# Attention, dense mixture and routed mixture on one core: the turn to the routed mixture is rearranged

## The chip, the cores and the metric

One core of a Trainium2 chip runs one program. TensorE (PE) multiplies, VectorE (DVE), ScalarE (ACT) and GpSimd (POOL) do the elementwise work, and SyncE (SP), ACT and POOL issue the DMAs. The metric is the device time of one execution in microseconds (us); less is better.

## What is computed

Three layers follow each other. Causal attention with a decay (batch 2, 8 heads, 576 positions, 64 per head) gives x, 1152 tokens of 512 numbers. A dense mixture runs every token through 4 experts. A routed mixture sends each token through at most one of 8 experts:

```python
def _moe_ref(x, domain_probs, w1, w2):            # N 1152, D 512, E 4, F 1024
    p = domain_probs / (domain_probs.sum(-1, keepdims=True) + 1e-09)
    for e in range(E):
        h = np.maximum(x @ w1[e], 0.0)
        out += p[:, e:e + 1] * (h @ w2[e])

def _moe2_ref(x, w_skip, w_gate, w1, w2):         # N 1152, D 512, E 8, F 1024
    do_compute = x @ w_skip > 0
    out = x.copy()
    xc = x[do_compute]
    e_idx = np.argmax(xc @ w_gate, axis=1)
    gate_w = softmax(xc @ w_gate)[rows, e_idx]
    for e in range(E):
        h = np.maximum(xc[e_idx == e] @ w1[e], 0.0)
        y[e_idx == e] = gate_w[...] * (h @ w2[e])
    out[do_compute] = xc + y
```

## The kernel before

**The stages.** Attention takes the first 200 us or so, the dense mixture runs until about 520, the end of the routing until 527, and the routed mixture until 628, where the last results go out by an indirect DMA.

**The dense mixture** works through 8 units u (an expert and a half of F, numbered 0 to 7), each for two groups of tokens: group g=0 holds tokens 0 to 511, g=1 the other 640. The up product (emit_up, L749 to L807) is a product of seven sums in the manner of Strassen; each operand of x is split in a high and a low half, `xsh[g]` and `xsl[g]`, which lie in SBUF for all units. The down product (emit_down L832, down_block L809 to L830) adds each block of 128 tokens into the accumulator `acc`; a quarter of a block is three matmuls `dn` (L818 to L820), and DVE adds the finished block to acc (L830).

**The last unit's down product** (L901) is mixed with the routing. The table `plan` (L836 to L841) names, for block n and quarter j, which step of the routing of which block t of tokens is emitted there. route1 issues ACT's stores of the finished block of acc into the DRAM buffers `xd` and `out` and, for t under 5, `xda` (store, L639 to L643), then transposes the block on PE (`xp`, L648) and copies it on ACT (`xt`, L649). route2 computes the logits on PE (`lg`, L655) and chooses the expert on DVE. route3 counts earlier tokens per expert on PE (`pf`, L683 and L685) and makes the slots and the one-hot matrix on DVE (L687 to L698). route4 adds the tokens into the slots' lists (`pids`, L704) and computes the weight of the choice on ACT (L716). `lg` and `pf` share a place in PSUM. The plan has a regular spacing for blocks 0 to 3 and entries of its own for blocks 4 to 7. ACT's stores use a ring of DMA lanes, so that a store also waits for an earlier one on its lane.

**The routed mixture's weights** are blocks of 1 MB (128 x 2048). SP loads most of them (`load_m`, L140 to L144, tiles `wm`) and POOL a few by indirect DMA (L1035 to L1042). The list `mpool` says which memory block i goes to, on a ring of 17: 0 is a free buffer of the dense weights (loaded with unit 7), 1 to 10 lie over the sums, weights and x operands of the dense up product, and 11 to 16 over other buffers of the dense mixture. load_m(1, 13) stands after unit 7's up product, when the pools of that memory are closed.

**The routed mixture** has per expert a tile of 64 slots (`Few`) and two further tiles for what is left over (`Many`). Zeroed rows `xe_1` to `xe_7` and `xo_0`, `xo_1` (L983 to L988) are filled from `xd` by POOL's indirect gathers (L592), whose empty slots keep the zeros. The first tile's rows `xs0` are gathered earlier from `xda`. Per tile, PE transposes the rows (`tpx`, L1054), ACT or DVE copies them (`xt`), PE multiplies up (L1061), ACT applies the relu (`hs`, L1064), PE transposes (`tp`, L1068) and multiplies down (`yp`, L1076). The zeroed rows lie over the memory of acc, so that their first writes wait until the stores of acc are done.

Of the kernel before, what the change touches and what calls it, by code (L numbers as in the profile page):

```python
# [7 lines left out]
F32 = mybir.dt.float32  # L8
# [10 lines left out]
P = 128  # L19
# [11 lines left out]
NS7 = 7  # L31
# [15 lines left out]
def kernel(  # L47
# [16 lines left out]
    def pool(stack, name, bufs=1, side="left", space=None):  # L64
        kw = dict(space=space) if space is not None else dict(side=side)
        return stack.enter_context(tc.tile_pool(name=name, bufs=bufs, reuse_waits="tile", **kw))

    const = pool(ctx, "const")
    dram = ctx.enter_context(tc.tile_pool(name="dram", bufs=1, space=DRAM))
    wrawu = pool(ctx, "wrawu", 1)  # L70
    upst = ExitStack()
    sumsp = pool(upst, "sums", 1)
    w1p = pool(upst, "w1a", 1)
# [26 lines left out]
    dps = const.tile([P, NB, E1], F32, name="dps")  # L100
    dsum = const.tile([P, NB], F32, name="dsum")
    wgs = const.tile([P, KD, E2 + 1], F32, name="wgs")
    xsh, xsl = [[xtp.tile([P, NS7, 2, GW[g]], F32R, name=f"x{c}_{g}") for g in range(2)] for c in "hl"]
    xtail = xop.tile([P, KD, S - 2 * GW[0]], F32, name="xtail")

    xd = dram.tile([N, DM], F32, name="xd")
# [33 lines left out]
    def load_m(i0, i1, eng=SY):  # L140
        for i in range(i0, i1):
            if chunks[i][1] < E2:
                w, a, e, h = ring(i)
                eng.dma_start(out=w, in_=(m1, m2)[a][e, h])  # L144

    def sub(eng, out, a, b):
        eng.tensor_tensor(out=out, in0=a, in1=b, op=ALU.subtract)  # L147
# [49 lines left out]
    with ExitStack() as at:  # L197
# [207 lines left out]
        def x_src(g, i, k):  # L405
            return x_parts(g, i, k // 2)[:, k % 2] if k in (0, 2, 3) else state["t", g, i][(4, 5, 1, 6).index(k)]

        def x_high(g, i, *ks):
            for k in ks:
                A.copy(out=xsh[g][:, k, i, :], in_=x_src(g, i, k))  # L410

        def x_low(eng, g, i, *ks):
            for k in ks:
                sub(eng, xsl[g][:, k, i, :], x_src(g, i, k), xsh[g][:, k, i, :].bitcast(F32))

        def x_sums(eng, g, i):
            t = xop.tile([P, 4, GW[1]], F32, tag="t", name=f"xs_{g}_{i}")
# [173 lines left out]
    def gather(xe, ix, table=xd, blocks=NB):  # L591
        G.indirect_dma_start(out=xe, out_offset=None, in_=table.rearrange("n (g c) -> (n g) c", g=2),  # L592
                             in_offset=bass.IndirectOffsetOnAxis(ap=ix, axis=0),
                             bounds_check=2 * blocks * P - 1, oob_is_err=False)

    outr = out.rearrange("n (g c) -> (n g) c", g=2)
    accp = pool(ctx, "accp", 1, "right")
    w1ps.append(pool(ctx, "w1b", 1, "right"))
    wrawd = pool(ctx, "wrawd", 1, "right")
    w2p = pool(ctx, "w2p", 1, "right")  # L600
    onehot = accp.tile([P, NB, P], BF16, name="onehot")
    xs0 = accp.tile([P, HD], F32, name="xs0")
    xt0 = accp.tile([P, HD], F32, name="xt0")
    pida = accp.tile([P, E2], F32, name="pida")
    idx0 = accp.tile([P, 1], I32, name="idx0")
    cnt = accp.tile([P, E2], F32, name="cnt")
    G.memset(xs0, 0.0)
    load_d(0)
    with tc.manual_schedule():
# [15 lines left out]
    UL = len(units) - 1  # L625

    with ExitStack() as mo:
        acc = pool(mo, "acc", 1, "right").tile([P, NB, DM], F32, name="acc")
        rt_p = pool(mo, "rt", 2, "right")
        hid_p = pool(mo, "hid", 1, "right")  # L630
        mid_p = pool(mo, "mid", 2, "right")

        macc = {}
        rt = {}
# [112 lines left out]
        hid = {}  # L747

        def emit_up(u, g, q, jobs):  # L749
            w, xh, xl, wt = GW[g], xsh[g], xsl[g], ws["u", u, q]  # L750
            hh, hl = hid[u, g]

            def bank(nm):
                return ps_p.tile([P, 512], F32, tag="ps", name=f"{nm}_{u}_{g}_{q}")[:, :w]

            def product(ps, a, b):
                for i in range(2):
                    T.matmul(out=ps, lhsT=wt[:, 0, a, i, :], rhs=xh[:, b, i, :], start=(i == 0), stop=False)  # L758
                    T.matmul(out=ps, lhsT=wt[:, 0, a, i, :], rhs=xl[:, b, i, :], start=False, stop=False)  # L759
                    T.matmul(out=ps, lhsT=wt[:, 1, a, i, :], rhs=xh[:, b, i, :], start=False, stop=(i == 1))  # L760
                if jobs:
                    jobs.pop(0)()

            def mid(nm):
                return mid_p.tile([P, GW[1]], F32, tag=nm, name=f"{nm}_{u}_{g}_{q}")[:, :w]

            def relu(c, r, h):
                j, cs = 2 * q + r, slice(h * w, h * w + w)
                A.activation(out=hh[:, j, cs], in_=c, func=AF.Relu)  # L769
                V.scalar_tensor_tensor(out=hl[:, j, cs], in0=c, scalar=0.0, in1=hh[:, j, cs].bitcast(F32),  # L770
                                       op0=ALU.max, op1=ALU.subtract)

# [63 lines left out]
        plan = {(5, 1): [(route1, 4)], (5, 3): [(route2, 4)], (6, 1): [(route1, 5)], (6, 2): [(route3, 4)],  # L836
                (6, 3): [(route4, 4)], (7, 0): [(route2, 5)], (7, 2): [(route1, 6)], (7, 3): [(route3, 5)],
                (8, 0): [(route2, 6)], (8, 1): [(route4, 5)], (8, 2): [(route1, 7)], (8, 3): [(route3, 6)]}
        for t in range(NX - 1):
            for n, j, fn in ((1, 1, route1), (2, 0, route2), (2, 3, route3), (3, 1, route4)):  # L840
                plan.setdefault((t + n, j), []).append((fn, t))  # L841

# [2 lines left out]
                fn(t)  # L845

        def hid_new(u, g):
            hid[u, g] = [hid_p.tile([P, 4, 2 * GW[g]], F32R, tag=f"h{c}{g}", name=f"h{c}_{u}_{g}") for c in "hl"]
# [11 lines left out]
        for u in range(UL + 1):  # L860
            jobs = prep(u)
            if u == UL:
                mpool[0] = wrawu, "raw"
                load_m(0, 1)
            hid_new(u, 0)
            emit_up(u, 0, 0, [])
            if u:
                emit_up(u, 0, 1, [])
                emit_down(u - 1, range(*GB[1]))
            hid_new(u, 1)  # L870
            down_new(u)
            emit_up(u, 1, 0, jobs[2])
            if u == 0:
                emit_up(u, 0, 1, [])
            emit_up(u, 1, 1, jobs[3])
            load_d(u + 1)
            if u == UL:
                break
# [12 lines left out]
        upst.close()  # L891
        mp = pool(ctx, "mp", 10)
        for k, x in enumerate([(mp, "m")] * 10 + [(w1ps[1], "w1"), (wrawd, "raw"), (w2p, "w2h"), (w2p, "w2l")]):
            mpool[k + 1] = x
        load_m(1, 13)
        ps_u = pool(mo, "ps_u", 3, space=PSUM)
        ps_d = pool(mo, "ps_d", 2, space=PSUM)
        ps_r = pool(mo, "ps_r", 1, space=PSUM)
# [28 lines left out]
        sel = hid_p.tile([P, 4, 2 * GW[0]], F32, tag="hl0", name="sel")[:, 0, 0:(NB - NX) * RT]  # L927
        sel = sel.rearrange("p (i c) -> p i c", i=NB - NX)

        def mine(t):  # L930
            m32 = rt[t]["m32"] = rtile([P, 1], "m32", t)
# [48 lines left out]
        weigh(NA - 1, NB)  # L980


    xe_p = pool(ctx, "xe", 1, "right")  # L983
    xes = [xs0] + [xe_p.tile([P, HD], F32, name=f"xe_{e}") for e in range(1, E2)]
    xos = [xe_p.tile([P, DM], F32, name=f"xo_{k}") for k in range(KO)]
    G.memset(xes[1], 0.0)
    for x in xes[2:] + xos:
        A.copy(out=x, in_=zero.to_broadcast([P, x.shape[1]]))  # L988
    xt_p = pool(ctx, "xt", 1, "right")
    wraw2 = pool(ctx, "wraw2", 2, "right")  # L990
    for k in range(15, RING):
        mpool[k] = wraw2, "raw"
    ps_m = pool(ctx, "ps_m", 1, space=PSUM)

    ys = [xt_p.tile([P, HD], F32, name=f"ys_{i}") for i in range(4)]
# [338 lines left out]
```

## Time and profile before

| | us |
|---|---|
| three runs | 632.54, 633.4, 635.96 |
| median | 633.4 |
| the profiled execution | 635.63 |
| its span in the profile | 633.8 |
| PE busy in the span | 603.2 (95%) |
| DVE, ACT, POOL busy | 332.5, 263.4, 322.2 |

The mean granted clock of PE is 0.973 of full speed. In the profile's picture of the span in 40 slices (15.8 us each) the busy shares of PE and its clock are level from slice 11 on, except around the last unit's down product and the start of the routed mixture, and in the same slices the DMA engines are at their limit. So the views by stretch and by engine are read there: 449 to 550 us.

### The profile page before, as it was taken

The page shows a single profiled execution, that of the slowest core. Times are in us where ns is not written, and L with a number is a line of the kernel's source. Part 1 is how long each engine was busy: PE and PEld are TensorE (multiplying, and loading weights), DVE is VectorE, ACT ScalarE, POOL GpSimd, SP SyncE. Part 2 cuts the span into 40 slices and gives each one's busy share as a digit, 9 for nine tenths or more (in the row PEclk, how much of TensorE's full clock was granted, in tenths as well). Part 3 has the DMA queues.
Part 4 walks back from the last instruction along what each step waited for, and adds up shares of the span by engine and source line. Part 5 has one row for each costly group of instructions (what it writes and reads, how often), then busy time and mean ns, then how long its engine had stood idle before and what let it go on. Part 6 is the DMA issues. An engine that isn't in the chain of part 4 may idle for free. (4 is left out here: it accounts for less than half of the span.)

```text
span 633.8 us, 10699 instructions
## 1 busy us (share of the span) xinstructions
PE 603.2 (95%) x3961; PEld 497.2 (78%) x3961; DVE 332.5 (52%) x885; ACT 263.4 (42%) x664; POOL 322.2 (51%) x349
## 2 busy tenths in 40 slices
PE   8998999899999999999999999999999795899996
PEld 5786878798898898898898898898897572455674
DVE  6876877665453453453453453453455573411653
ACT  5677888564243243243243243243241112111661
POOL 4869997589167167167167177177140002332411
PEclk7999999899999999999999999999999888899998
DMA  6676651310112011012011012011019999599910
GB/s 205 218 261 226 199 160 28 125 68 26 43 66 67 1 68 66 2 67 66 1 67 67 1 68 67 0 67 68 1 66 341 405 373 406 193 417 420 379 72 23
DMA packets 20423, 86.59 MB, mean 137 GB/s; under 512 B 3086, under 2 KB 4120, under 8 KB 13200
## 3 DMA queue, kind: packets, MB, share of 16 engines
q1 hardware_dynamic: 14816, 69.52, 30.2%
q0 software_dynamic: 2240, 10.32, 4.2%
q10 hardware_dynamic: 3312, 6.03, 2.5%
q8 instruction: 32, 0.52, 0.3%
q14 instruction: 23, 0.19, 0.1%
HBM read 79.44 MB, written 7.64 MB: 137 GB/s over the span
## 5 line engine op out<-in xcount | busy, mean ns | idle before, releaser
L758 PE MATMUL p<-xh,w 128*128 128x256 f32 (+1 forms) x448 | 132.7, 296 | 0.9 <-DVE u L780 0.4
L760 PE MATMUL p<-xh,w 128*128 128x256 f32 (+1 forms) x448 | 132.2, 295 | 0.0
L759 PE MATMUL p<-xl,w 128*128 128x256 f32 (+1 forms) x448 | 132.2, 295 | 0.0
L818 PE MATMUL dn<-w2h,hh 128*128 128x512 f32 x288 | 116.6, 405 | 0.0
L819 PE MATMUL dn<-w2l,hh 128*128 128x512 f32 x288 | 114.5, 398 | 0.0
L820 PE MATMUL dn<-w2h,hl 128*128 128x512 f32 x288 | 114.5, 397 | 0.0
L830 DVE SCALAR_TENSOR_TENSOR acc<-dn,dps,acc 128x512 f32<-128x512 f32 (+1 forms) x64 | 47.4, 742 | 100.0 <-PE dn L820 100.0
L147 POOL TENSOR_TENSOR w2l<-rawd,w2h 128x512 fp32r<-128x512 f32 x32 | 40.6, 1299 | 98.1 <-ACT w2h L192 98.1
L758 PEld LDWEIGHTS p<-xh,w 128*128 128x128 f32 x448 | 84.6, 189 | 2.7 <-ACT m L784 0.8
L759 PEld LDWEIGHTS p<-xl,w 128*128 128x128 f32 x448 | 84.6, 189 | 0.7
L760 PEld LDWEIGHTS p<-xh,w 128*128 128x128 f32 x448 | 84.6, 189 | 0.0
L820 PEld LDWEIGHTS dn<-w2h,hl 128*128 128x128 f32 x288 | 54.5, 189 | 13.3
L819 PEld LDWEIGHTS dn<-w2l,hh 128*128 128x128 f32 x288 | 54.5, 189 | 11.5
L818 PEld LDWEIGHTS dn<-w2h,hh 128*128 128x128 f32 x288 | 54.4, 189 | 11.4
L192 ACT CAST w2h<-rawd 128x512 fp32r<-128x512 f32 x32 | 18.3, 624 | 87.2 <-PE dn L820 87.2
L147 POOL TENSOR_TENSOR hl<-m,hh 128x256 fp32r<-128x256 f32 (+1 forms) x32 | 25.9, 808 | 49.7 <-ACT hh L776 49.7
L770 DVE SCALAR_TENSOR_TENSOR hl<-p,hh 128x256 fp32r<-128x256 f32 (+1 forms) x64 | 29.4, 459 | 35.6 <-ACT hh L769 35.6
L147 POOL TENSOR_TENSOR w<-ws,w 128x512 fp32r<-128x512 f32 x32 | 41.0, 1302 | 4.1 <-ACT w L166 4.1
L288 ACT ACTIVATE e<-sn,mn 128x128 f32<-128x128 f32 (+3 forms) x64 | 35.5, 556 | 12.0 <-DVE mn L285 11.8
L769 ACT ACTIVATE hh<-p 128x256 fp32r<-128x256 f32 (+1 forms) x64 | 26.1, 408 | 28.7 <-DVE p L780 28.7
L775 ACT ACTIVATE m<-m 128x256 f32<-128x256 f32 (+1 forms) x32 | 14.3, 445 | 52.7 <-DVE m L780 52.7
L285 DVE CUSTOM_DVE_ANT_0 sn<-s,bias 128x128 f32<-128x128 f32 (+3 forms) x64 | 29.8, 486 | 5.8 <-PE s L282 2.7
(259 smaller groups left out, 1146.8 us busy)
## 6 DMA issues: line engine op xcount, KB each, us to landing
wm<-in_m SPq DMA_DIRECT2D x32, 1024.0 KB, 8.7
rawu<-in_w SPq DMA_DIRECT2D x8, 1024.0 KB, 4.8
rawd<-in_w SPq DMA_DIRECT2D x8, 1024.0 KB, 4.7
qk<-in_qk SPq DMA_DIRECT2D x7, 640.0 KB, 6.1
qk<-in_qk SPq DMA_DIRECT2D x7, 576.0 KB, 4.0
bias<-nbd SPq DMA_DIRECT2D x14, 288.0 KB, 6.0
v<-in_v SPq DMA_DIRECT2D x8, 320.0 KB, 3.0
bias<-nbd SPq DMA_DIRECT2D x16, 144.0 KB, 5.8
```

The lines of the kernel that those rows point to most:

```text
L147: eng.tensor_tensor(out=out, in0=a, in1=b, op=ALU.subtract)
L285: V.tensor_tensor_reduce(out=sneg[:, :w], in0=ps[:, :w], in1=bi[:, h, :w], scale=-0.125, scalar=3.0e38, op0=ALU.add, op1=ALU.min, accum_ou ...
L288: A.activation(out=e[:, :w], in_=sneg[:, :w], func=AF.Exp, bias=mn, scale=-1.0, accum_out=st["sum"][:, 2 * i + h:2 * i + h + 1])
L758: T.matmul(out=ps, lhsT=wt[:, 0, a, i, :], rhs=xh[:, b, i, :], start=(i == 0), stop=False)
L759: T.matmul(out=ps, lhsT=wt[:, 0, a, i, :], rhs=xl[:, b, i, :], start=False, stop=False)
L760: T.matmul(out=ps, lhsT=wt[:, 1, a, i, :], rhs=xh[:, b, i, :], start=False, stop=(i == 1))
L769: A.activation(out=hh[:, j, cs], in_=c, func=AF.Relu)
L770: V.scalar_tensor_tensor(out=hl[:, j, cs], in0=c, scalar=0.0, in1=hh[:, j, cs].bitcast(F32), op0=ALU.max, op1=ALU.subtract)
L818: T.matmul(out=ps, lhsT=hh[:, j, ks], rhs=wh[:, j, :], start=(j == 0), stop=False)
L819: T.matmul(out=ps, lhsT=hh[:, j, ks], rhs=wl[:, j, :], start=False, stop=False)
L820: T.matmul(out=ps, lhsT=hl[:, j, ks], rhs=wh[:, j, :], start=False, stop=(j == 3))
L830: V.scalar_tensor_tensor(out=a, in0=ps[:, c0:c1], scalar=pe, in1=a, op0=ALU.mult, op1=ALU.add)
```

## The change

Three parts.

1. **Weight blocks earlier.** The x operands of group 0 become four tiles `xa_0` to `xa_3`; the first three are 8 KB a partition each, just a weight block, in a pool of their own. `mpool` sends blocks 1 to 3 there and block 4 to the dense down weights' buffer; blocks 5 to 11 take a pool of 7 blocks where there was one of 10. load_m(1, 4) is emitted after the last up product of group 0 in unit 7, load_m(4, 5) after unit 7's last up product, and load_m(5, 13) where load_m(1, 13) was.
2. **Zeroed rows.** `rows` and `rowo`, in the memory of the hidden layer of group 0 (pool hida), are cleared by two POOL memsets at plan place (6, 2); the routed mixture's gathered rows and four result tiles `ys` lie in them. The memset and the eight copies of zeros after the routing are gone. Pools are opened in another order, so that xt and the last two weight blocks of the ring (`wraw2`) lie over acc now.
3. **Routing.** The plan's regular spacing holds for blocks 0 to 6.

```diff
+    xa = [xap.tile([P, 4, 2, GW[0]], F32R, tag=f"a{i}", name=f"xa_{i}") for i in range(3)]
+    xa.append(xtp.tile([P, 2, 2, GW[0]], F32R, name="xa_3"))
+    xb = [xtp.tile([P, NS7, 2, GW[1]], F32R, name=f"xb_{c}") for c in "hl"]
...
-        plan = {(5, 1): [(route1, 4)], (5, 3): [(route2, 4)], (6, 1): [(route1, 5)], (6, 2): [(route3, 4)],
...
-        for t in range(NX - 1):
+        def cleared(t):
+            rows = hida_p.tile([P, 8, HD], F32, tag="hh0", name="rows")
+            rowo = hida_p.tile([P, 8, HD], F32, tag="hl0", name="rowo")
+            G.memset(rows[:, 1:E2], 0.0)
+            G.memset(rowo[:, 0:2 * KO], 0.0)
+            xes.extend([xs0] + [rows[:, e] for e in range(1, E2)])
+            xos.extend(rowo[:, 2 * k:2 * k + 2].rearrange("p a c -> p (a c)") for k in range(KO))
+            ys.extend(rowo[:, 2 * KO + i] for i in range(4))
+
+        plan = {(8, 1): [(route1, 7)], (6, 2): [(cleared, 0)]}
+        for t in range(NA):
             for n, j, fn in ((1, 1, route1), (2, 0, route2), (2, 3, route3), (3, 1, route4)):
                 plan.setdefault((t + n, j), []).append((fn, t))
...
             if u == UL:
-                mpool[0] = wrawu, "raw"
+                for k, x in enumerate([(wrawu, "raw")] + [(xap, f"a{i}") for i in range(3)] + [(wrawd, "raw")]):
+                    mpool[k] = x
                 load_m(0, 1)
             hid_new(u, 0)
             emit_up(u, 0, 0, [])
             if u:
                 emit_up(u, 0, 1, [])
+                if u == UL:
+                    load_m(1, 4)
                 emit_down(u - 1, range(*GB[1]))
...
             emit_up(u, 1, 1, jobs[3])
+            if u == UL:
+                load_m(4, 5)
+                break
             load_d(u + 1)
...
-        mp = pool(ctx, "mp", 10)
-        for k, x in enumerate([(mp, "m")] * 10 + [(w1ps[1], "w1"), (wrawd, "raw"), (w2p, "w2h"), (w2p, "w2l")]):
-            mpool[k + 1] = x
-        load_m(1, 13)
+        mp = pool(ctx, "mp", 7)
+        for k, x in enumerate([(mp, "m")] * 7 + [(w1ps[1], "w1"), (w2p, "w2h"), (w2p, "w2l")]):
+            mpool[k + 5] = x
+        load_m(5, 13)
...
-    xe_p = pool(ctx, "xe", 1, "right")
-    xes = [xs0] + [xe_p.tile([P, HD], F32, name=f"xe_{e}") for e in range(1, E2)]
-    xos = [xe_p.tile([P, DM], F32, name=f"xo_{k}") for k in range(KO)]
-    G.memset(xes[1], 0.0)
-    for x in xes[2:] + xos:
-        A.copy(out=x, in_=zero.to_broadcast([P, x.shape[1]]))
```

On PE, in block 6 of the last down product, this is what stands in a row before. In the names, the number behind `lg` or `pf` is the block t, and dn_7_6 is unit 7, block 6.

```order
L818 MATMUL dn_7_6_5938<-w2h_7_5445,hh_7_1_5443 128x512
L819 MATMUL dn_7_6_5938<-w2l_7_5446,hh_7_1_5443 128x512
L820 MATMUL dn_7_6_5938<-w2h_7_5445,hl_7_1_5444 128x512
L655 MATMUL lg_4_5905<-wgs_99,xt_4_5878 128x9 x4
L683 LDWEIGHTS upper_76
L683 MATMUL pf_3_5923<-mall_86,upper_76 128x8
L685 LDWEIGHTS ones_77
L685 MATMUL pf_3_5923<-macc_2_5847,ones_77 128x8
```

After the change the logits of block 4 stand there followed by matmuls dn.

```order
L667 MATMUL lg_4_5930<-wgs_102,xt_4_5901 128x9 x4
L831 MATMUL dn_7_6_5929<-w2h_7_5460,hh_7_1_5458 128x512
L832 MATMUL dn_7_6_5929<-w2l_7_5461,hh_7_1_5458 128x512
L833 MATMUL dn_7_6_5929<-w2h_7_5460,hl_7_1_5459 128x512
L716 LDWEIGHTS onehot_2050
L716 MATMUL pids_5646<-perm_93,onehot_2050 128x8
L716 LDWEIGHTS onehot_2050
L716 MATMUL pids_5646<-perm_93,onehot_2050 128x8
L660 MATMUL xp_5_5968<-ident_78,acc_2107 128x128 x4
```

The counting step `pf_3`, which followed `lg_4` at once, now stands ahead of it with two quarters' worth of other rows between; every block from 1 to 7 has the same row of steps.

On ACT, at the turn to the routed mixture, these rows stand between the weights of the choice and the first relu before.

```order
L716 ACTIVATE ex_6_6223,gs_6_6224<-d_8_6206 128x8
L988 COPY xe_6250<-zero 128x256
L988 COPY xe_6251<-zero 128x256
L988 COPY xe_6252<-zero 128x256
L988 COPY xe_6253<-zero 128x256
L988 COPY xe_6254<-zero 128x256
L988 COPY xe_6255<-zero 128x256
L988 COPY xo_6256<-zero 128x512
L988 COPY xo_6257<-zero 128x512
```

After the change the first relu follows at once.

```order
L728 ACTIVATE ex_6_6235,gs_6_6236<-d_8_6218 128x8
L1079 ACTIVATE hs_0_6275<-up_0_6292 128x512
```

The eight copies are gone from ACT and nothing has taken their place there.

On POOL, the rows after the last work for the dense mixture were these before.

```order
L592 DMA xs0_2043<-xda_106,idx0_2046 128x256
L986 MEMSET xe_1_6249 128x256
L592 DMA xe_1_6249<-xd_105,idx_91 128x256
L592 DMA xe_2_6250<-xd_105,idx_91 128x256
L592 DMA xe_3_6251<-xd_105,idx_91 128x256
```

After the change they are these.

```order
L852 MEMSET rows_5977 128x1792
L853 MEMSET rowo_5978 128x1024
L601 DMA xs0_2051<-xda_111,idx0_2054 128x256
L601 DMA rows_5977<-xd_110,idx_94 128x256 x7
```

The memset moved ahead of the gather of `xs0` and grew from 256 to 1792 and 1024 columns. A gather of `rows` waits for the stores into `xd` and for the slots' list, the ones of before also for the copies of zeros.

## Rows read from the trace of the kernel before

**Rows 1.** Stretches: length, busy us (instructions) by engine, PE's clock, DMA share, GB/s.
```profile
449.00:469.50 20.50, 20.50 (x107) 17.75 (x106) 7.78 (x15) 5.64 (x13) 6.66 (x7) 1.00 0.00 1
...
495.80:503.60 7.80, 4.78 (x29) 3.74 (x29) 3.73 (x25) 0.79 (x3) 0.00 (x0) 1.00 1.03 414
503.60:510.50 6.90, 6.05 (x21) 3.76 (x21) 3.53 (x21) 1.09 (x5) 0.00 (x0) 0.51 1.01 417
...
531.00:537.30 6.30, 0.00 (x1) 0.00 (x0) 0.50 (x3) 3.46 (x9) 2.31 (x3) 0.77 1.00 420
537.30:546.40 9.10, 6.96 (x40) 4.13 (x42) 0.42 (x1) 0.74 (x2) 4.98 (x5) 0.60 0.28 94
546.40:628.00 81.60, 81.08 (x516) 48.37 (x512) 35.14 (x66) 29.17 (x46) 19.96 (x19) 1.00 0.71 285
```

**Rows 2.** PE timeline, last down product: start, duration, line, tile [idle before <-releaser].
```profile
498.56 0.39 PE L819 MATMUL dn<-w2l,hh 128*128 128x512 f32 x1
...
500.41 1.06 PE L655 MATMUL lg<-wgs,xt 128*128 128x9 f32 x8 [1.22 <-ACT xt L649]
503.28 0.18 PE L683 MATMUL pf<-mall,upper 128*128 128x8 bf16 x1 [1.81 <-DVE d L677]
...
503.66 0.63 PE L819 MATMUL dn<-w2l,hh 128*128 128x512 f32 x1
...
505.56 1.12 PE L648 MATMUL xp<-ident,acc 128*128 128x128 f32 x4 [0.84 <-DVE acc L830]
```

**Rows 3.** ACT timeline, the store of block 4 into xda and its copy.
```profile
499.35 0.33 ACTq L643 DMA_DIRECT2D xda<-acc  x1
499.77 0.59 ACT L649 COPY xt<-xp 128x512 f32<-128x512 f32 x1 [6.09 <-DMA xda<-acc]
```

**Rows 4.** PE timeline, the start of the routed mixture.
```profile
527.03 3.65 PE L1061 MATMUL up<-wm,xt 128*64 128x512 f32 x16 [0.32 <-ACT ex L716]
...
537.33 1.12 PE L1068 MATMUL tp<-ident,hs 128*128 128x128 f32 x4 [6.32 <-ACT hs L1064]
...
541.17 5.35 PE L1076 MATMUL yp<-wm,ht 128*64 128x256 f32 x32
...
555.19 3.62 PE L1076 MATMUL yp<-wm,ht 128*64 128x256 f32 x32
```

**Rows 5.** ACT and POOL timelines, the same stretch.
```profile
521.23 0.33 ACTq L640 DMA_DIRECT2D xd<-acc  x1
...
533.82 1.93 ACT L988 COPY xe<-zero 128x256 f32<-128x256 f32 x6 [6.45 <-DMA out<-acc]
...
536.69 0.58 ACT L1064 ACTIVATE hs<-up 128x512 f32<-128x512 f32 x1
539.06 0.37 ACT L1070 COPY ht<-tp 128x256 f32<-128x256 f32 x1 [1.79 <-DVE ht L1069]
...
533.99 0.31 POOL L986 MEMSET xe<- 128x256 f32 x1 [18.73 <-DMA out<-acc]
534.79 1.01 POOL L592 DMA_INDIRECT xe<-xd,idx  x1 [0.50 <-POOL xe L986]
```

**Rows 6.** Landings: the last xd store, load 14 (issued 520.13), the seven gathers.
```profile
DMA to landing us min/median/max: 8.1/8.1/8.1
...
wm<-in_m SPq DMA_DIRECT2D x1, 1024.0 KB, 8.8
...
DMA to landing us min/median/max: 2.5/2.8/5.7
```

**Rows 7.** DVE timeline: one step alone, and beside POOL's gather of 514.08.
```profile
503.73 0.29 DVE L691 TENSOR_SCALAR onehot<-slotn,rank 128x128 bf16<-128x128 f32 x1
...
514.75 0.54 DVE L691 TENSOR_SCALAR onehot<-slotn,rank 128x128 bf16<-128x128 f32 x1
```

**Rows 8.** POOL's weight fetch issued at 579.15 (landing), and its user on ACT.
```profile
DMA to landing us min/median/max: 15.6/15.6/15.6
...
595.41 1.98 ACT L1105 CAST wh<-wm 128x1024 fp32r<-128x1024 f32 x2
```

More of the change, by code (lines that the diff above doesn't have):

```diff
@@ L70 @@
     wrawu = pool(ctx, "wrawu", 1)
+    xap = pool(ctx, "xa", 1)
     upst = ExitStack()
@@ L102 @@
     wgs = const.tile([P, KD, E2 + 1], F32, name="wgs")
-    xsh, xsl = [[xtp.tile([P, NS7, 2, GW[g]], F32R, name=f"x{c}_{g}") for g in range(2)] for c in "hl"]
+    xa = [xap.tile([P, 4, 2, GW[0]], F32R, tag=f"a{i}", name=f"xa_{i}") for i in range(3)]
+    xa.append(xtp.tile([P, 2, 2, GW[0]], F32R, name="xa_3"))
+    xb = [xtp.tile([P, NS7, 2, GW[1]], F32R, name=f"xb_{c}") for c in "hl"]
     xtail = xop.tile([P, KD, S - 2 * GW[0]], F32, name="xtail")
@@ L144, in load_m, with xs @@
                 eng.dma_start(out=w, in_=(m1, m2)[a][e, h])
+    def xs(c, g, k):
+        if g:
+            return xb[c][:, k]
+        n = c * NS7 + k
+        return xa[n // 4][:, n % 4]
     def sub(eng, out, a, b):
@@ L409, in x_high @@
             for k in ks:
-                A.copy(out=xsh[g][:, k, i, :], in_=x_src(g, i, k))
+                A.copy(out=xs(0, g, k)[:, i, :], in_=x_src(g, i, k))
         def x_low(eng, g, i, *ks):
             for k in ks:
-                sub(eng, xsl[g][:, k, i, :], x_src(g, i, k), xsh[g][:, k, i, :].bitcast(F32))
+                sub(eng, xs(1, g, k)[:, i, :], x_src(g, i, k), xs(0, g, k)[:, i, :].bitcast(F32))
         def x_sums(eng, g, i):
@@ L594, in gather @@
                              bounds_check=2 * blocks * P - 1, oob_is_err=False)
+    xes, xos, ys = [], [], []
     outr = out.rearrange("n (g c) -> (n g) c", g=2)
@@ L600 @@
     w2p = pool(ctx, "w2p", 1, "right")
+    hida_p = pool(ctx, "hida", 1, "right")
     onehot = accp.tile([P, NB, P], BF16, name="onehot")
@@ L606 @@
     cnt = accp.tile([P, E2], F32, name="cnt")
+    sel = accp.tile([P, NB - NX, RT], F32, name="sel")
     G.memset(xs0, 0.0)
@@ L627 @@
     with ExitStack() as mo:
+        hidb_p = pool(mo, "hidb", 1, "right")
+        mid_p = pool(mo, "mid", 2, "right")
         acc = pool(mo, "acc", 1, "right").tile([P, NB, DM], F32, name="acc")
         rt_p = pool(mo, "rt", 2, "right")
-        hid_p = pool(mo, "hid", 1, "right")
-        mid_p = pool(mo, "mid", 2, "right")
         macc = {}
@@ L749, in emit_up @@
         def emit_up(u, g, q, jobs):
-            w, xh, xl, wt = GW[g], xsh[g], xsl[g], ws["u", u, q]
+            w, wt = GW[g], ws["u", u, q]
             hh, hl = hid[u, g]
@@ L756, in product @@
             def product(ps, a, b):
+                xh, xl = xs(0, g, b), xs(1, g, b)
                 for i in range(2):
-                    T.matmul(out=ps, lhsT=wt[:, 0, a, i, :], rhs=xh[:, b, i, :], start=(i == 0), stop=False)
-                    T.matmul(out=ps, lhsT=wt[:, 0, a, i, :], rhs=xl[:, b, i, :], start=False, stop=False)
-                    T.matmul(out=ps, lhsT=wt[:, 1, a, i, :], rhs=xh[:, b, i, :], start=False, stop=(i == 1))
+                    T.matmul(out=ps, lhsT=wt[:, 0, a, i, :], rhs=xh[:, i, :], start=(i == 0), stop=False)
+                    T.matmul(out=ps, lhsT=wt[:, 0, a, i, :], rhs=xl[:, i, :], start=False, stop=False)
+                    T.matmul(out=ps, lhsT=wt[:, 1, a, i, :], rhs=xh[:, i, :], start=False, stop=(i == 1))
                 if jobs:
@@ L847, in hid_new @@
         def hid_new(u, g):
-            hid[u, g] = [hid_p.tile([P, 4, 2 * GW[g]], F32R, tag=f"h{c}{g}", name=f"h{c}_{u}_{g}") for c in "hl"]
+            hid[u, g] = [(hida_p, hidb_p)[g].tile([P, 4, 2 * GW[g]], F32R, tag=f"h{c}{g}", name=f"h{c}_{u}_{g}") for c in "hl"]
         def prep(u):
@@ L875 @@
             emit_up(u, 1, 1, jobs[3])
+            if u == UL:
+                load_m(4, 5)
+                break
             load_d(u + 1)
-            if u == UL:
-                break
             up_high_s(u + 1, 0)
@@ L926 @@
         xsel = ps_u.tile([P, 512], F32, tag="u", name="xsel")
-        sel = hid_p.tile([P, 4, 2 * GW[0]], F32, tag="hl0", name="sel")[:, 0, 0:(NB - NX) * RT]
-        sel = sel.rearrange("p (i c) -> p i c", i=NB - NX)
         def mine(t):
@@ L993 @@
     ps_m = pool(ctx, "ps_m", 1, space=PSUM)
-    ys = [xt_p.tile([P, HD], F32, name=f"ys_{i}") for i in range(4)]
     yos = [xt_p.tile([P, DM], F32, name=f"yo_{k}") for k in range(KO)]
```

2 lines of the change are left out of this document (removed).

## The prediction

> **What bounds the kernel now.** I read the table of stretches first, for PE's busy time, its clock and the DMA share [rows 1]. From 546.4 to 628.0 PE works 81.08 of 81.6 us at full clock: PE sets the time there, and work taken from another engine gains nothing. In 449 to 469.5 PE is busy throughout while the DMA engines move 1 GB/s: bandwidth lies idle. Two stretches are weak.
>
> The first is the last down product. From 495.8 to 503.6 PE works 4.78 of 7.80 us, and from 503.6 to 510.5 it works 6.05 of 6.90 at a clock of 0.51, the lower of its two levels (1.2 of 2.4 GHz) [rows 1]. PE's timeline names three waits: 1.22 us before the logits of block 4, 1.81 before the counting step behind them, 0.84 before a transpose. From then on a matmul dn takes 0.63 us where it took 0.39 [rows 2]. The second wait is for DVE's choice on the very logits just made, since `pf` needs the place in PSUM of `lg`. The first is for ACT's copy, which stood 6.09 us behind a store of the same block that waited for its lane until 499.35 [rows 3]. The DMA share is 1.03 and 1.01 here [rows 1].
>
> The second is the start of the routed mixture. PE ends the first up product at 530.68 (527.03 and 3.65) and then does nothing from 531.0 to 537.3, and from 537.3 to 546.4 it works at a mean clock of 0.60 [rows 1, 4]. It waits 6.32 us for the first relu [rows 4], which stands in ACT's queue behind the copies of zeros; these waited 6.45 us until 533.82, when the last store of acc had landed [rows 5]. The first down product then takes 5.35 us, where a later one takes 3.62 [rows 4].
>
> **Part 3, the even spacing.** At block 6 the counting step now comes ahead of the logits, not directly behind them, so the 1.81 us go, and with the pattern of the earlier blocks the 0.84 after it. What the first stretch loses now is 7.80 − 4.78 = 3.02 and 6.90 − 6.05 = 0.85 of idle time, together 3.87 (the three waits add to the same), and the low clock: by the clock 6.05 × (1 − 0.51) = 3.0, by the matmul 6.05 × (1 − 0.39/0.63) = 2.3. I take 2.7 between them: 6.6 in all [rows 1, 2]. The first wait stays: ACT's order has the store of block 4 into xda ahead of the copy as before, and its lane is freed by an earlier store, whose transfer runs among the same saturated DMAs. The logits come only some 0.1 later in PE's queue, so I keep 1.1 of the 1.22. Gain 6.6 − 1.1 = 5.5. If the clock falls all the same after this one wait, only the 1.81 goes, 1.8 us; if the earlier loads free the lane too, all 6.6.
>
> **Part 2, the zeroed rows.** The ACT copies and the wait for acc's stores go from ahead of the relu, which can then run directly behind the up product (530.7), and PE's transpose with it, 0.64 after the relu's start as in before (536.69 to 537.33), at about 531.3. The copy of its result followed 1.73 us later (539.06 against 537.33) and takes 0.37 [rows 4, 5], so the down product could start at 533.4 at the pace of then, and near 532.5 at full clock. What is late next is the gather for expert 1, which stands between on PE. It now waits for the last store into xd and the slots' list alone. That store was issued at 521.23 and landed 8.1 us later, at 529.3; a gather takes 2.5 to 5.7 to land, 2.8 in the median [rows 5, 6]. 529.5 + 2.8 gives 532.3. I take 532.8 for the start of the down product in the times of before, where it was 541.17: 8.4 earlier; and since PE then idles some 1 to 2 us and not 6.3, I take full clock, 3.62 and not 5.35, 1.7 more [rows 4]. Counting the overlap at its end, 546.4 becomes 536.4 or 536.5: gain 9.9. Bounds: 10.8 if the down product follows at 531.9; 4.6 if the gather takes its longest (landing at 535.5 to 535.8) and the clock is low (536.4 + 5.35 = 541.75).
>
> The new memsets are 7 and 4 times the 256 columns that took 0.31 [rows 5]: some 2.1 and 1.2 us on POOL, an estimate. They stand where POOL has no work until the gather for `xs0` at 514. POOL alone is touched, so I take 0. If their memory is freed late, they are still ready 20 us ahead of the first gather. If DVE is held while they run, its routing step comes up to 2.1 late, and PE behind it; a step of DVE beside POOL's gather took 0.54 where it takes 0.29 alone [rows 7], a loss of 0.25. The row is the nearer: 0, up to 2.1 for the range.
>
> The Trainium skill ("SBUF — State Buffer", Who interferes with whom) says that VectorE in its two-port modes and GpSimd take turns at one pair of ports, and that the loser waits for the whole instruction. That speaks against long memsets beside the routing. The row agrees in kind: the longer DVE step overlaps a POOL instruction. By the rule the sum would be up to 2.1 us less.
>
> **Part 1, the earlier blocks.** Four blocks of 1 MB move up: three to where the DMA engines idle (449 to 469.5), one to its end. They cost PE nothing, since they lie on SP's queue, and POOL's and ACT's queues aren't passed. In the saturated stretch some 4 MB less stand ahead of the stores at its end. In the routed mixture the turn comes 15 us earlier for PE, and the DMA engines there are 0.71 busy [rows 1]: at 285 GB/s, 15 us are 4.3 MB, just what was loaded earlier. So the SP blocks come in time by about the same margin. POOL's own fetches are tighter: one issued at 579.15 landed after 15.6, at 594.75, and its split began at 595.41 [rows 8], 0.7 us of slack. They are issued by PE's progress, so they move with it. 0, up to a loss of 3.
>
> **Sum.** 5.5 + 9.9 + 0 + 0 = 15.4. The profiled execution's own time is 635.63 (span 633.8), so 620.2 for it; it was the second slowest figure beside the three runs, whose median is 633.4. From the median: **618.0 us**.
>
> **The rivals.**
>
> R1, the gather becomes the wait. The last store lands late behind the loads, PE idles 4 us and falls to the low clock. For: DMA share 1.00 in this stretch, 8.1 us to land, and a first gather of 5.7 [rows 1, 6]. Against: fewer loads are queued now, and the gather no longer waits for the `out` stores. Gain 5.5 + 4.6: 623.3.
>
> The Trainium skill ("DMA: Bandwidth & Descriptors", Queues, rings and completion order) says that a semaphore's increment lands only after every earlier write of that DMA engine, across its queues. The rows agree: load 14, ahead of the last xd store on another queue, landed at 528.9 and the store at 529.3 [rows 6]. By that the store is no faster than the load ahead of it, however small, which supports R1 and the 529.3 I used.
>
> R2, the first stall stays. One wait of 1.1 with late lanes before the next is enough to lower the clock. For: PE waits first for the lane, not for the plan [rows 2, 3]. Against: the clock was 1.00 until 503.6, through the 1.22, and fell after the 1.81 [rows 1, 2]. Gain 1.8 + 9.9: 621.7.
>
> R3, weight blocks come late in the routed mixture, since PE arrives 15 us earlier: the 0.7 of slack is used up and PE waits some 3 us [rows 8]. 621.0.
>
> R4, slower. The wait of R3 recurs at each expert, and each time PE falls to the low clock: a ratio of 5.35/3.62 = 1.48 [rows 4], so 81.6 us would become up to 121, a loss of 39 [rows 1]. It decides over the gain from 15.4/39 = 0.4 of the routed mixture on; at three quarters of it, 30 − 15.4 slower: 648. Against: the DMA share of 0.71.
>
> R5, the change doesn't do what it says: the wait for acc's stores moves from the zeroed rows to the first copy of transposed rows, which now lies over acc. In before the last `out` store was down by 533.8; the copy comes near 533, so at most 1 or 2 us: 619 to 620.
>
> **How the numbers follow.** Forecast 0.55 (616 to 620.2, the upper end where the profiled execution's surplus of 2.2 over the median sat in the two stretches), R1 0.20, R2 0.13, R3 0.07, R5 0.03, R4 0.02. The range goes from 615.0 (6.6 + 10.8 = 17.4 gives 616.0, and the lowest run of before was 0.9 under its median) to 623.5, which takes in R1's time, R2, R3 and R5; what is left out is R4, sums of two rivals and some of R1's tail. About 0.5%, 3.2 us, is what a measurement of this kernel can tell from no change. All cases but R4 gain over 9, so faster 0.95; for several rivals together 0.03 for the same; slower 0.02.
>
> **What would show it.** In the profile after: no idle before `pf` of block 3 and full clock in the last down product (part 3), one wait near 1 us before the logits of block 4; the relu directly behind the first up product, down product of 3.6 us, and gap at the turn under 3 us (part 2); DMA work in the idle stretch before 470 and PE busy in all but 1 us of the routed mixture (part 1). The forecast is wrong if the clock is low in either stretch, if DVE steps double beside the memsets, or if splits of weights wait for fetches.

## The result

The kernel after takes 618.07 us in the median (617.69 to 619.29), the kernel before 633.73 beside it: a ratio of 0.975 (95% interval 0.972 to 0.978). The forecast was 618.0. That the sum came out is luck: the turn to the routed mixture gave 5.6 us where 9.9 were forecast, and a term that the prediction doesn't have, 4.8 us in the dense mixture, took the place of what was missing.

Stretches of the profiled execution after (span 617.6, own time 619.29), the columns as in [rows 1]:

```profile
449.00:469.50 20.50, 20.50 (x117) 18.72 (x116) 8.70 (x17) 5.47 (x12) 6.73 (x6) 1.00 0.44 177
495.80:503.60 7.80, 7.80 (x51) 6.13 (x52) 6.66 (x39) 1.37 (x4) 0.00 (x0) 1.00 1.02 408
503.60:510.50 6.90, 6.48 (x45) 5.03 (x43) 5.52 (x31) 0.82 (x4) 1.18 (x1) 1.00 0.47 144
...
516.00:526.00 10.00, 6.12 (x39) 2.86 (x39) 2.90 (x16) 2.13 (x10) 5.85 (x6) 0.96 0.78 287
526.00:531.00 5.00, 5.00 (x32) 2.76 (x31) 0.61 (x2) 0.00 (x0) 1.14 (x2) 0.74 1.03 406
...
537.00:612.00 75.00, 74.30 (x468) 45.67 (x466) 29.79 (x42) 28.30 (x44) 18.82 (x18) 1.00 0.69 283
```

The last down product is whole: PE works 7.80 of 7.80 us at a clock of 1.00 where it worked 4.78, and the stretch of clock 0.51 is gone. DMA work now stands in the idle stretch before 469.5 (share 0.44). The turn is not whole: between 516 and 526 PE works 6.12 of 10.00, and the mean clock is 0.74 behind it.

Where the 16.2 us between the two spans lie is read from four places that both programs pass. First, ACT's timeline: the first and the last store into xd, and the store of block 4 into xda. Before:

```profile
479.18 0.35 ACTq L640 DMA_DIRECT2D xd<-acc  x1
...
521.23 0.33 ACTq L640 DMA_DIRECT2D xd<-acc  x1
```

After:

```profile
475.25 0.34 ACTq L652 DMA_DIRECT2D xd<-acc  x1
...
494.18 0.33 ACTq L655 DMA_DIRECT2D xda<-acc  x1
494.55 0.59 ACT L661 COPY xt<-xp 128x512 f32<-128x512 f32 x1 [4.95 <-DVE g L738]
...
510.69 0.33 ACTq L652 DMA_DIRECT2D xd<-acc  x1
```

The first store comes 3.93 us earlier, before any edited step of PE's order has run. From the first to the last it took 42.05 and takes 35.44: 6.61 won. The copy of block 4 still stands right behind its store into xda, but it ends at 495.14, and PE reaches the logits of block 4 at 495.21 without a wait.

Then PE's timeline at the turn:

```profile
516.44 3.65 PE L1076 MATMUL up<-wm,xt 128*64 128x512 f32 x16 [0.32 <-ACT ex L728]
...
520.85 0.66 PE L1083 MATMUL tp<-ident,hs 128*128 128x128 f32 x4 [0.43 <-ACT hs L1079]
524.64 0.41 PE L1069 MATMUL tpx<-ident,rows 128*128 128x128 f32 x2 [3.14 <-DMA rows<-xd,idx]
524.98 5.36 PE L1091 MATMUL yp<-wm,ht 128*64 128x256 f32 x32
530.17 1.89 PE L1076 MATMUL up<-wm,xt 128*64 128x512 f32 x8
```

The relu no longer holds PE (0.43 for 6.32 in [rows 4]). The gather of expert 1's rows does, for 3.14, and the first down product takes 5.36, as long as before. From the first up product to the first down product it was 541.17 − 527.03 = 14.14 and is 524.98 − 516.44 = 8.54: 5.60 won. Together 3.93 + 6.61 + 5.60, and 0.05 between the last store and the first up product, are the 16.2. Behind 530 the two programs run alike.

POOL's timeline has the new memsets and the first gather, and the tile's views the landings (the time from a DMA's issue until its data has arrived) of the last store into xd and of that gather:

```profile
486.51 1.59 POOL L852 MEMSET rows<- 128x1792 f32 x1 [14.03 <-issue]
488.03 0.95 POOL L853 MEMSET rowo<- 128x1024 f32 x1
...
518.62 1.00 POOL L601 DMA_INDIRECT rows<-xd,idx  x1 [12.75 <-DVE g L738]
```

```profile
DMA to landing us min/median/max: 7.1/7.1/7.1
...
DMA to landing us min/median/max: 5.9/5.9/5.9
```

The store lands at 517.8, the gather issues 0.8 later and lands after 5.9, at 524.5, where the forecast took the 2.8 of [rows 6]. The DVE held by a memset is to be seen too, one step beside the second memset and four us later:

```profile
488.45 0.56 DVE L690 TENSOR_SCALAR perm<-mall,tokp 128x8 bf16<-128x8 bf16 x1
...
492.82 0.22 DVE L690 TENSOR_SCALAR perm<-mall,tokp 128x8 bf16<-128x8 bf16 x1
```

The step ends at 489.01, the memset at 488.98. No instruction of PE waited for it.

### The profile page after: what moved, and what is told of

Read it like the earlier page. It is cut to its first block, busy times and chain, and to the rows that moved or that the text cites. A ratio compares the mean times of both kernels' runs of the same rounds, so it can differ in the third digit from the quotient of the medians.

```text
span 617.6 us, 10693 instructions
## 1 busy us (share of the span) xinstructions
PE 595.2 (96%) x3961; PEld 495.4 (80%) x3961; DVE 332.7 (54%) x885; ACT 260.6 (42%) x656; POOL 323.8 (52%) x350
## 5 line engine op out<-in xcount | busy, mean ns | idle before, releaser
L831 PE MATMUL dn<-w2h,hh 128*128 128x512 f32 x288 | 114.2, 397 | 0.0
L833 PE MATMUL dn<-w2h,hl 128*128 128x512 f32 x288 | 112.5, 391 | 0.0
L832 PE MATMUL dn<-w2l,hh 128*128 128x512 f32 x288 | 112.2, 390 | 0.0
L771 PE MATMUL p<-xb_h,w 128*128 128x320 f32 x224 | 69.4, 310 | 0.7 <-DVE u L793 0.5
L773 PE MATMUL p<-xb_h,w 128*128 128x320 f32 x224 | 69.2, 309 | 0.0
L772 PE MATMUL p<-xb_l,w 128*128 128x320 f32 x224 | 69.2, 309 | 0.0
L771 PE MATMUL p<-xa,w 128*128 128x256 f32 x224 | 63.2, 282 | 0.1
L773 PE MATMUL p<-xa,w 128*128 128x256 f32 x224 | 62.9, 281 | 0.0
L772 PE MATMUL p<-xa,w 128*128 128x256 f32 x224 | 62.9, 281 | 0.0
L771 PEld LDWEIGHTS p<-xb_h,w 128*128 128x128 f32 x224 | 42.0, 188 | 1.6 <-DVE u L793 0.8
L771 PEld LDWEIGHTS p<-xa,w 128*128 128x128 f32 x224 | 42.5, 190 | 0.7 <-DVE hl L783 0.3
L772 PEld LDWEIGHTS p<-xa,w 128*128 128x128 f32 x224 | 42.5, 190 | 0.3
L773 PEld LDWEIGHTS p<-xa,w 128*128 128x128 f32 x224 | 42.5, 190 | 0.0
```

What stands on the lines that cost most here:

```text
L771: T.matmul(out=ps, lhsT=wt[:, 0, a, i, :], rhs=xh[:, i, :], start=(i == 0), stop=False)
L772: T.matmul(out=ps, lhsT=wt[:, 0, a, i, :], rhs=xl[:, i, :], start=False, stop=False)
L773: T.matmul(out=ps, lhsT=wt[:, 1, a, i, :], rhs=xh[:, i, :], start=False, stop=(i == 1))
L831: T.matmul(out=ps, lhsT=hh[:, j, ks], rhs=wh[:, j, :], start=(j == 0), stop=False)
L832: T.matmul(out=ps, lhsT=hh[:, j, ks], rhs=wl[:, j, :], start=False, stop=False)
L833: T.matmul(out=ps, lhsT=hl[:, j, ks], rhs=wh[:, j, :], start=False, stop=(j == 3))
```

## Experiments

In what follows a ratio is to the kernel before on the same chip; 0.001 is 0.63 us. The time of one program varies by some us between executions, most of it ahead of the first store, which came between 472.11 and 476.46 in eight traces of programs that are alike up to there. PE's clock rises at different times in the first 30 us: the kernel after was at 0.67 from 10 to 20 us and 0.83 from 20 to 30 where that of before was at 0.55 and 1.00, and reached the dense mixture 0.88 later. So the small terms are read from the traces, place by place.

### What took 4 us before the first store

Along the order of PE's 3961 matmuls the kernel after falls 0.88 behind in attention and then wins 4.8 evenly through the dense mixture, all of it in the down product. Its matmuls dn follow each other at 0.2333 us before and at 0.2272 after, in each unit. Nothing in the diff changes them. What it changes is where their operands lie: the stationary operand (`hh`, `hl`, loaded ahead of the matmul) began 96 bytes over a multiple of 128 and begins at one now, while the moving one (`w2h`, `w2l`) began at a multiple in both. Twelve matmuls lie between the two rows, before and after:

```profile
311.62 0.40 PE L818 MATMUL dn<-w2h,hh 128*128 128x512 f32 x1
...
314.42 0.40 PE L818 MATMUL dn<-w2h,hh 128*128 128x512 f32 x1
```

```profile
311.79 0.39 PE L833 MATMUL dn<-w2h,hl 128*128 128x512 f32 x1
...
314.51 0.39 PE L833 MATMUL dn<-w2h,hl 128*128 128x512 f32 x1
```

2.80 and 2.72 for the twelve. The modelled duration hardly tells it (0.40 and 0.39); the distance of the starts does.

The kernel after with the hidden layer 32 bytes further, `a_shift`:

```diff
+    pool(ctx, "pad", 1, "right").tile([P, 8], F32, name="pad")
     hida_p = pool(ctx, "hida", 1, "right")
...
+        pool(mo, "pad2", 1, "right").tile([P, 8], F32, name="pad2")
         mid_p = pool(mo, "mid", 2, "right")
```

> The kernel after with hh and hl moved by 32 bytes, everything else at addresses of the same remainder by 64 as in it. Theory A, the address of the stationary operand by 64 bytes sets the spacing: 0.234 instead of 0.227 and 5 us more, time about 623.3. Rival B, the address is nothing: 618.

Ratio 0.983 (0.979 to 0.987), that is 5 us of the gain gone, and the old spacing:

```profile
311.70 0.39 PE L835 MATMUL dn<-w2h,hl 128*128 128x512 f32 x1
...
314.50 0.39 PE L835 MATMUL dn<-w2h,hl 128*128 128x512 f32 x1
```

The same edit with 16 columns, 64 bytes further, `a_shift64`:

> The kernel after with hh and hl moved by 64 bytes and everything else at the same remainders. Theory, the remainder of the stationary operand's address by 128 counts: a spacing of 0.230 us, as in the kernel before with the 32-byte tile, between the 0.227 of the kernel after and the 0.234 of a shift by 32. Rival, the remainder by 64 alone counts: 0.227, and the 0.230 there had another cause.

```profile
311.74 0.39 PE L833 MATMUL dn<-w2h,hh 128*128 128x512 f32 x1
...
314.49 0.39 PE L833 MATMUL dn<-w2h,hh 128*128 128x512 f32 x1
```

2.75 for twelve; over each unit a mean of 0.2291. So three steps: 0.2272 at 0, 0.2291 at 64 and 0.2333 at 96 over a multiple of 128. (Its 617.78 us is a single execution; its turn is read further down.)

The kernel before with the 32-byte tile ahead of its hidden layer, `b_align`, which brings it from 96 to 64:

```diff
+        pool(mo, "pad", 1, "right").tile([P, 8], F32, name="pad")
         hid_p = pool(mo, "hid", 1, "right")
```

> The kernel before with one edit: an unused tile of 32 bytes a partition ahead of the hidden layer's pool, so that hh and hl begin at a multiple of 64 bytes (before: 32 over one). Theory A, this address is why the down product's matmuls in the kernel after follow each other every 0.227 us instead of 0.234: the spacing falls to 0.227 and 864 matmuls give 864 x 0.0063 = 5.4 us, time about 628.3. Rival B, the difference comes from other contents of the change (where acc, x or the down weights lie): spacing 0.234, time unchanged within 0.5 us of 633.5.

```profile
311.70 0.39 PE L819 MATMUL dn<-w2h,hh 128*128 128x512 f32 x1
...
314.44 0.39 PE L819 MATMUL dn<-w2h,hh 128*128 128x512 f32 x1
```

2.74, the spacing of 64 over, and a ratio of 0.995 (0.992 to 0.998), 3 us. The forecast of 5.4 took the remainder by 64 for the whole of it; 64 of 128 is the middle step.

Does it hold for the up product, whose x operands begin 32 bytes over a multiple of 128? `a_align` moves these, the up weights of the even halves and most routed blocks:

```diff
-    rowoff = const.tile([P, 1], F32, name="rowoff")
-    tokp = const.tile([P, 1], F32, name="tokp")
+    offs = const.tile([P, 2], F32, name="offs")
+    rowoff, tokp = offs[:, 0:1], offs[:, 1:2]
```

> The kernel after with two 4-byte constants in one tile, which moves the x operands, the up weights of the even halves and the routed blocks from 32 over a multiple of 64 bytes to a multiple. Theory A, a moving operand's address counts as the stationary one's: the up product's matmuls (0.117 to 0.120 us for 256 columns, 0.147 for 320) get some 0.003 to 0.006 us shorter each, 1344 of them give 4 to 8 us, and the leftover tiles' matmuls of 512 columns go from 0.234 to 0.227, time about 610 to 614. Rival B, only the stationary operand counts: 0.120 becomes 0.117 in half of the 256-column matmuls, about 1 us, time about 617.

Ratio 0.980 (0.977 to 0.984): no gain. The matmuls of 256 columns follow at 0.120 in all units, where in the kernel after those of the odd halves (weights at a multiple of 128, x 32 over one) followed at 0.117; those of 320 stay at 0.147. Both theories fall here. What address is good depends on both operands; for the up product the rule stays open.

### The even spacing

The kernel before with the new plan alone, `b_even`:

```diff
-        plan = {(5, 1): [(route1, 4)], (5, 3): [(route2, 4)], (6, 1): [(route1, 5)], (6, 2): [(route3, 4)],
...
-        for t in range(NX - 1):
+        plan = {(8, 1): [(route1, 7)]}
+        for t in range(NA):
```

> The kernel before with the evenly spaced routing alone (part 3). Theory A, the spacing is what cleared the last down product: the three waits and the low clock go, last store into xd 6.6 us earlier than in the kernel before, time about 627. Rival B, the earlier weight blocks cleared it: the wait for the store of block 4 into xda stays at 499.3, the clock falls after it, and only 1.8 us are won, time about 632. Rival C, both are needed: about 1.1 us of wait stay and full clock holds, 5.5 us won, time about 628.

ACT's stores and PE's waits of some length:

```profile
479.25 0.34 ACTq L640 DMA_DIRECT2D xd<-acc  x1
...
499.20 0.33 ACTq L643 DMA_DIRECT2D xda<-acc  x1
...
515.82 0.33 ACTq L640 DMA_DIRECT2D xd<-acc  x1
```

```profile
PE tp L1066 <- ACT hs L1062: 7.8, 1, 7.8
PE tpx L1052 <- DMA xe<-xd,idx: 2.4, 1, 2.4
PE lg L655 <- ACT xt L649: 0.8, 1, 0.8
```

From the first store to the last 36.57: 5.48 won, with one wait of 0.8 left for the xda store. That is rival C of its expectation and the prediction's working (5.5 with 1.1 left). But the ratio is 0.995 (0.993 to 0.998), 2.9 us: the wait for the relu has grown from 6.32 [rows 4] to 7.8. The copies of zeros wait for stores, and the stores go through DMA engines that are full (share 1.02) whether PE is early or not: the last store into `out`, issued 5.4 us earlier than in the kernel before, landed 2.1 us earlier (531.7 and 533.8). Part of a gain ahead of a full queue is given back at the queue.

The kernel after with the old plan, `a_oldplan`:

```diff
-        plan = {(8, 1): [(route1, 7)], (6, 2): [(cleared, 0)]}
-        for t in range(NA):
+        plan = {(5, 1): [(route1, 4)], (5, 3): [(route2, 4)], (6, 1): [(route1, 5)], (6, 2): [(cleared, 0), (route3, 4)],
...
+        for t in range(NX - 1):
```

> The kernel after with the routing plan of the kernel before (part 3 undone; the clearing of the rows stays at its place). Theory: the wait of the counting step on the logits of block 4 (1.8 us) and the low clock behind it come back, the last store into xd some 5.5 us later from the first one (42.0 instead of 35.4 us), about 623.5. Rival, the earlier blocks alone had cleared the stretch: no low clock, at most 1.8 us more, about 619.9.

```profile
PE tpx L1071 <- DMA rows<-xd,idx: 4.2, 1, 4.2
PE pf L695 <- DVE d L689: 1.8, 1, 1.8
PE xp L660 <- DVE acc L843: 1.0, 2, 0.8
PE lg L667 <- ACT xt L661: 0.9, 1, 0.9
```

```profile
500.00:505.00 5.00, 5.00 (x18) 3.46 (x19) 2.46 (x17) 1.09 (x5) 0.04 (x1) 0.50 0.47 179
```

The waits of 1.81 and 0.84 are back, the one before the logits is 0.9 where it was 1.22, and the low clock is back with them. Ratio 0.984 (0.978 to 0.991), 5.8 us of the gain gone; its interval and that of the result just touch. The way from first to last store took 44.99 there. All traces with the old plan took 40.85 to 44.99 (four of them, that of before 42.05), all with the new one 35.44 to 37.04 (ten); no other edit moves one from one group to the other.

### The zeroed rows, and the gather

Meant to undo parts 1 and 3, `a_p2only` (the old plan, and the edit of the next section). By its trace it undoes part 3 alone, since that other edit moved no load, as the next section shows:

> The kernel after with parts 1 and 3 undone: the zeroed rows off the accumulator's memory alone, with the memory layout that comes with them. Theory: the relu follows the first up product at once, but the last down product stalls as in the kernel before and the gather lands late: the turn gains 4 to 6 us, the layout 5 us, about 623 to 625. Rival, without the other two parts the gather lands as late as the copies of zeros ended and nothing is won at the turn: about 628.5.

Ratio 0.986 (0.979 to 0.992), 9.1 us, of which the down product's operands are 5: the rows' own place and the earlier blocks together give some 4 without the new plan. The new plan alone gave 2.9; with the operands' 5 that is 12, and the change gives 15.7. The last 4 would come from having the parts together, as `b_even` suggests from its side. This run's interval reaches 4 us to either side, so their size is not shown.

What would the turn give if the gather didn't wait? In the kernel after SP issues blocks 15 to 18 between 518.9 and 520.5, beside the gather of 518.62. `a_gather` puts them on ACT's queue, behind its copy of the gathered rows; `a_gather2` puts only 15 and 16 there:

```diff
-    load_m(15, NS + 2)
     tiles[0].up(0)
...
     tiles[1].x_in()
+    load_m(15, 17, A)
+    load_m(17, NS + 2)
     tiles[0].down()
```

> The kernel after with blocks 15 to 18 issued on ACT's queue behind its copy of expert 1's rows, so that no weight block is in flight while the first gather is. Theory R1, the gather waits behind the blocks: it lands in 2.5 to 3 us instead of 5.9, PE waits under 0.5 us instead of 3.1, the first down product runs at full clock (3.6 instead of 5.4 us), 4 to 5 us less: about 613.5. Rival, the seven gathers hold each other up, or the low clock has another cause: the landing stays near 5.9 and the time at 618 or, with the later blocks missing in the mixture, above it.

> As the run with blocks 15 to 18 behind expert 1's rows, but with 15 and 16 alone there and the others back on SP. Theory: the first down product at full clock and at once is worth some 3.7 us as it was there, and the 1.8 us that PE then waited for a late block stay away or shrink: 3 us less than the kernel after. Rival: blocks 17 and 18 are in flight during the gather and hold it up again, no gain.

PE's timeline of `a_gather2` and the landing of its first gather:

```profile
522.97 0.38 PE L1069 MATMUL tpx<-ident,rows 128*128 128x128 f32 x2
523.72 3.67 PE L1091 MATMUL yp<-wm,ht 128*64 128x256 f32 x32 [0.37 <-DVE ht L1084]
```

```profile
DMA to landing us min/median/max: 2.8/2.8/2.8
```

The gather lands in 2.8, PE does not wait for it, and the down product takes 3.67 at full clock. `a_gather` does the same (3.67) but gives it back. From the last store into xd to the first up product it took 7.13 us, where the kernel after took 5.75, at a clock of 0.50 (510.2 to 517.0), and later it waits for want of a block:

```profile
PE yp L1091 <- DMA wm<-in_m: 1.8, 1, 1.8
```

Its ratio is 0.975 (0.969 to 0.981), no gain to be measured. `a_gather2` has no such wait, and its ratio is 0.968 (0.965 to 0.971), 615.24 us, beside 619.85 for the kernel after on that chip (`after_again`, 0.973, 0.969 to 0.977). It is the fastest here; the two intervals overlap, so the 4.6 us are likely and not sure, while the traces have 4.6 at the turn itself (from the first up product to the first down product 5.65 us, where the kernel after took 8.54, and 1.7 less for the down product).

`a_shift64` shows the same with no edit at the turn. Its four loads stand where the kernel after has them, but at the end of its routing PE's clock was low (0.50 from 514.1 to 517.4), and the routing's last step on DVE ended later against the stores. The first of these loads waits for that step, and goes out 0.13 us behind its end in both kernels. So it went out 1.67 us behind the first gather, where it was 0.32 in the kernel after (518.62 and 518.94). POOL's and SP's timelines and the gather's landing there:

```profile
520.22 1.00 POOL L601 DMA_INDIRECT rows<-xd,idx  x1 [13.45 <-DVE gs L732]
...
521.89 0.33 SPq L147 DMA_DIRECT2D wm<-in_m  x1
...
DMA to landing us min/median/max: 2.8/2.8/2.8
```

PE did not wait for it, the down product took 3.67, and the turn 5.65 us, all as in `a_gather2`, where the first load went out 1.92 us behind the gather (519.80 and 521.72). In both the loads started before the gather had landed. So the loads cause the late landing, and a start some 1.5 us later is enough to avoid it. Two chains race here: the gather follows the last store's landing, the first load follows DVE's last step.

> The kernel after, unchanged, beside the next two on one chip, as their measure: a ratio to the kernel before of 0.975, as in the result.

### The earlier blocks

Meant to undo part 1, `a_late`, and once more beside `after_again` as `a_late_b`:

```diff
-                if u == UL:
-                    load_m(1, 4)
...
-                load_m(4, 5)
...
-        load_m(5, 13)
+        load_m(1, 13)
```

> The kernel after with blocks 1 to 4 loaded where the kernel before loaded them (part 1 undone, memory as in the kernel after). Theory, the earlier blocks only relieve the saturated stretch: the wait for the store of block 4 into xda (0.8 us before the logits) comes back, and with 4 MB more queued the last store into xd and the gather behind it land 3 to 5 us later, so that PE waits 6 to 8 us instead of 3.1 for expert 1's rows: 622 to 624. Rival, the blocks are hidden anyway: 618 to 619.

> Part 1 undone once more (blocks 1 to 4 loaded where the kernel before loaded them), in more rounds. By the trace of its first run, part 1 is worth the 0.6 us wait for the store of block 4 into xda, 0.3 more to the end of the routing and 1.2 us at the turn: 2 us more than the kernel after. Rival, it is hidden: within 1 us of it.

```profile
PE tpx L1066 <- DMA rows<-xd,idx: 3.1, 1, 3.1
PE lg L667 <- DVE rank L699: 0.4, 1, 0.4
```

The edit did not do what it was meant to. SP's first block behind block 0, in the kernel before, in the kernel after and in `a_late`:

```profile
469.48 0.33 SPq L144 DMA_DIRECT2D wm<-in_m  x1
...
445.76 0.33 SPq L147 DMA_DIRECT2D wm<-in_m  x1
...
446.36 0.33 SPq L147 DMA_DIRECT2D wm<-in_m  x1
```

That is 9.70 us ahead of the first store into xd in the kernel before, 29.49 in the kernel after and 29.50 in `a_late`; it is 29.50 in `a_late_b` and 29.49 in `a_p2only`. Where the loads are emitted moved none of them; what is left of part 1 as their reason is the memory of their own, which these runs keep. So the two runs are the kernel after once more, and their ratios of 0.973 (0.966 to 0.980) and 0.974 (0.970 to 0.978) agree with its 0.973 on the second chip.

In `a_late_b` PE waits as in the kernel after (3.1 for the gather, none for the xda store). The first `a_late` had a wait of 0.6 for that store, and `after_again` has it too, so that wait comes and goes between executions. What the earlier blocks are worth stays open. `b_even`, without parts 1 and 2, speaks for more than nothing: its last store into xd landed 12.8 us after its issue, where that of the kernel after, behind a stretch with a DMA share of 0.47, took 7.1.

## Why the prediction came out, step by step

**Part 3: right.** 5.5 forecast, 6.61 measured in the profiled pair, 5.48 with the plan alone; some 0.6 of the 6.61 are the operands' address again (96 matmuls dn, 0.0061 each). The counting step `pf_3` now stands one quarter ahead of `lg_4`, not two as said with the change, and that is enough. The step of the lane was right on the whole: a wait of 0 to 1.2 us stays in front of the logits of block 4. That this one wait does not bring the low clock back (against R2) held in every trace with the new plan: the clock is 1.00 from first to last store in all ten.

**Part 2: the step that failed is the landing of the gather.** The prediction took 2.8 us, the median of seven gathers that ran when the loads had just ended [rows 1, 6], and moved it to a place where four loads start beside it. It had the right row at hand: the first of the seven took 5.7. The start of the down product was forecast 8.4 earlier and came 5.6 earlier. The second step that failed hangs on it: with 3.14 us of waiting the clock fell, so 1.7 were not won. This is R1 in the main, given 0.20, with nearly its price: 4.6 there, 5.6 here. But R1 put the lateness on the last store, and that landed no later than forecast, 7.1 us after its issue where 8.1 were taken. By the prediction's own signs it was wrong here: the clock was low at the turn, the gap over 3 us and the down product 5.36. The sentence of the Trainium skill beside R1 ("DMA: Bandwidth & Descriptors", Queues, rings and completion order), that an increment lands only after every earlier write of its DMA engine, agrees as far as the rows go: the gather landed at 524.5, behind the load that SP issued at 518.94, while POOL was issuing the gather, and that landed at 523.7. No run shows the order within one engine.

**The memsets: right.** Some 2.1 and 1.2 us were estimated, 1.59 and 0.95 measured. One DVE step was 0.34 us longer, as the Trainium skill's rule on the shared ports says ("SBUF — State Buffer", Who interferes with whom), up to the memset's end. That step more than doubled (0.22 to 0.56), which the prediction had as a sign of being wrong. It cost PE nothing, so the row was the better guide to the size.

**Part 1: its price of nothing is not shown,** neither right nor wrong, since no run takes the earlier loads away. The mixture kept its blocks: PE works 74.30 of 75.00 us behind the turn, so R3 and R4 did not come.

**What was missing.** That a matmul's rate could change with the address of its operands was in no step. The diff showed that the pools moved, and the prediction asked of it only which waits follow. That term of 4.8 us, less 0.88 that the execution lost in attention, stands against the 4.3 us lacking at the turn. Without it the change would have come out near 623, at the edge of the range and at R1's time; the hit on the total is luck and says little for the sum.

## What to carry to other kernels

A gather's or a store's landing time belongs to what else the DMA engines move at that moment: take it from a row with the same load beside it, and if a small transfer gates the critical path, let the big ones start a little behind it. Here 1.7 and 1.9 us were enough, and holding all four back for longer made one of them late. Work won ahead of a full DMA queue is partly given back at the next wait on that queue, so look at what the stage behind waits for before adding gains up. When an edit moves memory, compare the distance between successive matmuls of unedited code in both traces before crediting the gain to the edit. And before reading a time as the worth of something undone, look in the trace whether it is undone: compare when the loads go out, not where they are written.

## What the hardware showed unasked

A 128x128x512 matmul of the dense down product (type fp32r) followed the next at 0.2272, 0.2291 or 0.2333 us as its stationary operand began 0, 64 or 96 bytes over a multiple of 128, with the moving one at a multiple: 2.7%, 5 us of this kernel. For 256 columns 0.117 and 0.120 were seen, with the shorter one where the weights began at a multiple of 128 and x 32 over one, so no simple rule covers both. After waits of 1.8 or 3.1 us PE's clock was at its lower level for stretches of 3.3 us (0.50 from 525.2 to 528.5 in the kernel after) to 13.6 us (0.50 from 499.4 to 513.0 in `a_oldplan`); after single ones of up to 1.2 us (the logits of block 4) it was not. But it also fell at the end of the routing where PE's last waits had been some 0.4 us: 0.50 from 510.2 to 517.0 in `a_gather`, from 516.8 to 523.5 in `b_even` and from 514.1 to 517.4 in `a_shift64`. So the waits alone do not tell when it falls.
